# Attention and routed experts on one core: row operations from GpSimd to VectorE, and a slots' table read in two parts

## The chip, the core and the metric

The kernel runs on one core of a Trainium2 chip, as one program. The metric is the device time of one execution in microseconds (us); the time of a kernel is the median of its runs.

## What is computed

The reference first computes a linear attention without softmax, on 8 batches and 8 heads with 576 tokens of width 64, normalises each output row by its root mean square and scales it by `g_norm`. The 4608 rows of 512 numbers then go through a layer of 8 experts: each token goes to the expert with its largest logit, an expert takes at most `capacity` (1152) tokens in order, and each kept token's result is weighted by its gate.

```python
kv = np.einsum('bhsd,bhse->bhde', k, v)
out = np.einsum('bhsd,bhde->bhse', q, kv)
rms = np.sqrt(np.mean(out * out, axis=-1, keepdims=True) + 1e-06)
x = (out / rms * g_norm)                      # as rows of 512
...
expert_idx = np.argmax(x @ w_gate, axis=1)    # tokens of an expert in order, up to capacity
h = np.maximum(np.einsum('ecd,edf->ecf', disp, w1), 0.0)      # 512 -> 1024
y = np.einsum('ecf,efd->ecd', h, w2)                          # 1024 -> 512
out[i] = gate_w[i] * y[expert_idx[i], pos[i]]
```

## The kernel before, in words

The program has two plans, emitted one after the other. A planner (`Plan`, L97) takes operations with a planned duration, a list of engines that may do them, dependencies, a key and rings of buffers (`Ring`, L82, with `Hold`s). It simulates the engines and places, at each step, the operation with the lowest key among those that can start first; `late` moves an operation's earliest start back. The order that it finds is the order of each engine's instructions. The engines then run in that order, each waiting only for its real dependencies, so an instruction that waits holds up all that is behind it on its engine. GpSimd's and SP's DMA issues are part of their orders.

**First plan: attention and routing.** For each of the 8 batches TensorE makes k-v products and the outputs, ScalarE and VectorE copy them out of PSUM, and `route` (L866) finds each token's expert and its position there. With a product (`enter`, L1007) it writes the token's number into a table in PSUM, `tab`: column = expert and block of 128 positions (48 columns, once for the high and once for the low bits), partition = position within the block. `x_dram` gets the unnormalised rows with the row's factor and gate. After the third batch one expert is picked (`pick`, L1058) and its weights are loaded and split. After the fifth batch `early_slots` (L1146) reads the table (`read_table`, L1094) for that expert's first 384 slots, and `early_products` (L1241) computes their first expert layer. `finish` (L1274) reads the table again after the last batch, cuts the indices of the first expert's other slots (`slots`, L634: a register load, then a copy of the expert's six columns of `gidx_tab`, the rows to gather, and of `sidx_tab`, the rows to write) and ranks the experts by their number of tokens (`rank_experts`, L1071), so that each of the following experts gets a fixed budget of slots (704, 672, 640, 624, 592, 576, 560, 512).

`read_table` has eight operations of VectorE over 128x48: two put high and low bits together, one (L1098) sets slots beyond the capacity to 0, and `slot_rows` (L312) makes from token + 1 the row to gather (0 where the slot is empty) and the row to write (beyond the last row where it is empty).

**Second plan: the experts.** `rows_beside` (L1577) prepares the rows of expert r + 1 while expert r is computed: an indirect DMA issued by GpSimd gathers 128 rows (`xg`, L438, four buffers), `norm` (L442) multiplies them by their factors into `xm`, ScalarE rounds `xm` to f16 (`pair_high`, L469), `pair_low` (L474) makes the f16 rest, and a transposing DMA on SP's queue (L481) writes both into `xs`. For the second expert `norm` may be on VectorE or GpSimd; for the third expert on it is on GpSimd, as `pair_low` is for all. `weights` (L1526) loads an expert's two weight matrices in four parts each (SP's queue, L326) and splits them into f16 high and low parts: VectorE takes the largest magnitude of each of 8 pieces (L342, `am`), `most` reduces them and multiplies by `gcol` for the first matrix (L352), TensorE turns the column (`across`, L355, tile `pt_max`), VectorE reduces it (L359), TensorE spreads the number to all partitions (`back`, L362), VectorE makes the power of two (`scale`, L364 to L371), then ScalarE writes the high parts (L376) and VectorE the low parts (L382, `w1l` and `w2l`). `products` (L1612) computes an expert: eight groups of products into `hp` (L530, two buffers in PSUM), ScalarE's `hh` (L535), VectorE's `hl` (L538), then the second layer by blocks of 128 rows (L576, narrow ones L585 to L596), ScalarE's scaling into `ysb` (L601, three buffers) and GpSimd's indirect DMA to the output (L606). `hl` and other operations of the expert at hand have the key of one expert before, and `pt_max` has the lowest key of all (FIRST).

During the last expert VectorE runs the steps of `plan_rest` (L1331, 68 places for them), which prepare a part that is only run when an expert has more tokens than its budget.

## Time and profile before

| | us |
|---|---|
| median of 3 runs | 569.93 (567.73 to 570.16) |
| the profiled execution | 566.6 |
| its span, first to last instruction | 564.8 |
| TensorE busy | 520.2 (92%) |
| VectorE busy | 382.5 (68%) |
| ScalarE busy | 252.7 (45%) |
| GpSimd busy | 207.1 (37%) |
| mean granted TensorE clock | 0.981 of full |

The profile's lines name the engines PE (TensorE's products; PEld its weight loads), DVE (VectorE), ACT (ScalarE), POOL (GpSimd) and SP (SyncE; SPq its DMA queue). L576 is line 576 of the kernel before. `out<-in` are tile names, followed by shapes; `x8` counts instructions that were merged into one line. A bracket at the end of a line tells how long the engine had been idle before it and what ended the wait. Durations of neighbouring instructions overlap slightly, so the busy time of a merged line is less than their number times the duration of one.

### The profile page before, as it was taken

The numbers are of one execution on the slowest core, as the hardware profiler recorded it, in microseconds if no ns is written. First come the engines' busy times: TensorE is split into PE (matmuls) and PEld (weight loads), VectorE is DVE, ScalarE is ACT, GpSimd is POOL, SyncE is SP. The second block draws the span as 40 slices with busy tenths as digits, with TensorE's granted clock in tenths as the row PEclk, the third lists the DMA queues.
The fourth block names the chain that finished last, engine by engine and source line by source line (L and its number), as shares of the span: only waits on it lengthen the run. The fifth ranks groups of instructions, "written<-read, shape, count | busy, mean of one in ns | idle before, by whom it ended". The sixth has DMA issues, their size and how long they took to land.

```text
span 564.8 us, 12345 instructions
## 1 busy us (share of the span) xinstructions
PE 520.2 (92%) x4727; PEld 343.2 (61%) x4727; DVE 382.5 (68%) x978; ACT 252.7 (45%) x508; POOL 207.1 (37%) x233
## 2 busy tenths in 40 slices
PE   4989897978979997998999999999999999999995
PEld 4878786855536564544664575487467648745442
DVE  4468899899949979999997286367729606721200
ACT  1748684876313661644633526252544525202210
POOL 3011013552255684755225640644373171012011
PEclk9979996999999998999999999999999999999999
DMA  8999999592277687795938562664666151001001
GB/s 278 376 354 301 384 390 373 176 317 96 96 232 254 144 302 166 201 306 132 277 109 236 112 224 66 169 171 161 167 140 214 39 114 39 1 38 40 0 30 40
DMA packets 78020, 102.60 MB, mean 182 GB/s; under 512 B 43222, under 2 KB 51414, under 8 KB 76932
## 3 DMA queue, kind: packets, MB, share of 16 engines
q1 hardware_dynamic: 69600, 70.43, 42.5%
q0 software_dynamic: 7776, 31.30, 15.6%
q8 instruction: 39, 0.64, 0.5%
q14 instruction: 25, 0.20, 0.1%
q10 hardware_dynamic: 580, 0.02, 0.1%
HBM read 73.13 MB, written 20.61 MB: 166 GB/s over the span
## 4 chain that ended last, share of the span: by engine, by line
PE 26%; issue 16%; DMA 5%; DVE 3%; POOL 1%; ACT 1%; POOLq 0%; DVEq 0%; ACTq 0%
PE yp L576 12%; PE hp L530 12%; DMA out_dram<-ysb,si 5%; DVE w2l L382 1%; PE yp L585 1%; POOL xg L438 1%; DVE hl L538 1%; ACT w1h L376 0%; ACT w2h L376 0%; POOL xm L446 0%; POOLq L1652 0%; POOL pair L476 0%; POOL out_dram L606 0%; PE pt_max L355 0%; PE pt_max L362 0%
## 5 line engine op out<-in xcount | busy, mean ns | idle before, releaser
L530 PE MATMUL hp<-xs,w1h 128*128 128x320 f16 (+6 forms) x896 | 134.4, 301 | 5.1 <-DVE hl L538 4.5
L530 PEld LDWEIGHTS <-w1h 128*128 128x128 f16 x960 | 93.4, 98 | 47.1 <-issue 8.8
L576 PEld LDWEIGHTS <-hh 128*128 128x128 f16 x560 | 54.4, 98 | 65.5 <-issue 2.9
L606 POOL DMA_INDIRECT out_dram<-ysb,si x41 | 42.8, 1043 | 137.3 <-ACT ysb L601 99.6
L535 ACT ACTIVATE hh<-hp 128x320 f16<-128x320 f32 (+7 forms) x64 | 40.8, 638 | 114.5 <-PE hp L530 111.9
L342 DVE TENSOR_REDUCE am<-raw 128x1 f32<-128x512 f32 x120 | 75.6, 673 | 4.1 <-DMA raw<-in_moe_w_dram 3.8
L530 PE MATMUL hp<-xs,w1l 128*128 128x320 f16 (+6 forms) x448 | 72.0, 301 | 0.0
L538 DVE SCALAR_TENSOR_TENSOR hl<-hp,hh 128x320 f16<-128x320 f32 (+7 forms) x64 | 47.2, 737 | 32.9 <-ACT hh L535 32.8
L476 POOL TENSOR_TENSOR pair<-xm,pair 128x512 f16<-128x512 f32 (+5 forms) x35 | 44.7, 1278 | 66.5 <-ACT pair L472 61.8
L576 PE MATMUL yp<-w2h,hh 128*128 128x512 f16 x272 | 64.4, 379 | 0.8 <-ACT ysb L601 0.8
L576 PE MATMUL yp<-w2l,hh 128*128 128x512 f16 x272 | 64.6, 379 | 0.0
L576 PE MATMUL yp<-w2h,hl 128*128 128x512 f16 x272 | 64.3, 379 | 0.0
L601 ACT ACTIVATE ysb<-yp,ysc 128x512 f32<-128x512 f32 (+5 forms) x40 | 27.3, 684 | 82.4 <-PE yp L576 73.1
L382 DVE SCALAR_TENSOR_TENSOR w2l<-raw,sw,w2h 128x512 f16<-128x512 f32 x64 | 53.8, 885 | 10.7 <-ACT w2h L376 9.9
L530 PEld LDWEIGHTS <-w1l 128*128 128x128 f16 x480 | 46.9, 98 | 19.5
L438 POOL DMA_INDIRECT xg<-x_dram,gi x41 | 42.3, 1031 | 40.1 <-DVE gi L640 27.0
L382 DVE SCALAR_TENSOR_TENSOR w1l<-raw,sg,w1h 128x512 f16<-128x512 f32 x64 | 47.5, 797 | 0.9 <-ACT w1h L376 0.8
L576 PEld LDWEIGHTS <-hl 128*128 128x128 f16 x280 | 27.0, 98 | 31.9
L823 PE MATMUL op<-kv_bd,qt 128*128 128x144 f32 x256 | 42.6, 310 | 3.7 <-ACT qt L676 1.3
L376 ACT ACTIVATE w2h<-raw,sw 128x512 f16<-128x512 f32 x62 | 39.8, 711 | 5.2 <-DVE p2t L307 2.1
L376 ACT ACTIVATE w1h<-raw,sg 128x512 f16<-128x512 f32 x60 | 38.3, 711 | 7.2 <-DVE sg L371 7.1
L823 PEld LDWEIGHTS op<-kv_bd,qt 128*128 128x128 f32 x256 | 36.7, 206 | 6.0 <-ACT qt L676 2.2
(246 smaller groups left out, 688.7 us busy)
## 6 DMA issues: line engine op xcount, KB each, us to landing
raw<-in_moe_w_dram SPq DMA_DIRECT2D x64, 512.0 KB
k_sb<-in_k_dram SPq DMA_DIRECT2D x16, 576.0 KB
v_sb<-in_v_dram SPq DMA_DIRECT2D x16, 576.0 KB
x_dram<-o_sb POOLq DMA_DIRECT2D x8, 1152.0 KB
q_sb<-in_q_dram SPq DMA_DIRECT2D x16, 512.0 KB
x_dram<-o_sb POOLq DMA_DIRECT2D x8, 144.0 KB
q_sb<-in_q_dram SPq DMA_DIRECT2D x32, 32.0 KB
xg<-x_dram,gi POOLq DMA_INDIRECT x41
```

Of the source, the lines that this page charges most:

```text
L342: nc.vector.tensor_reduce(out=am()[:, p:p + 1], in_=raw[:, sl(p)], axis=AX.X, op=ALU.max, apply_absolute_value=True)
L376: nc.scalar.activation(wh[:, sl(p)], raw[:, sl(p)], AF.Copy, scale=z["s"])
L382: nc.vector.scalar_tensor_tensor(out=wl[:, sl(p)], in0=raw[:, sl(p)], scalar=z["s"], in1=wh[:, sl(p)], op0=ALU.mult, op1=ALU.subtract)
L438: nc.gpsimd.indirect_dma_start(out=self.xg[i][0:n], out_offset=None, in_=x_dram[0:self.rows, :], in_offset=bass.IndirectOffsetOnAxis(ap=se ...
L476: nc.gpsimd.tensor_tensor(out=pair[0:n, 1], in0=self.xm[i][0:n], in1=pair[0:n, 0], op=ALU.subtract)
L530: nc.tensor.matmul(self.view(hp)[:, u], lhsT=w[:, c, j * P:(j + 1) * P], rhs=x[:, c, u * hw:(u + 1) * hw], start=(t == 0 and c == 0), stop ...
L535: nc.scalar.activation(self.out(self.hh, j), self.view(hp), AF.Relu)
L538: nc.vector.scalar_tensor_tensor(out=self.out(self.hl, j), in0=self.view(hp), scalar=0.0, in1=self.out(self.hh, j), op0=ALU.max, op1=ALU.s ...
L576: nc.tensor.matmul(yp[0:n, 0:DM], lhsT=h[:, j, o:o + n], rhs=w[:, j, :], start=(m == 0), stop=(m == len(self.terms) - 1))
L601: nc.scalar.activation(self.ysb[0:n], yp[0:n, 0:DM], AF.Copy, scale=self.ysc[0:n, i:i + 1])
L606: nc.gpsimd.indirect_dma_start(out=out[:, :], out_offset=bass.IndirectOffsetOnAxis(ap=self.sidx[0:n, col:col + 1], axis=0), in_=ysb[0:n], ...
L823: nc.tensor.matmul(y, lhsT=qt.t[:, i * P:(i + 1) * P], rhs=kv2[:, half * HH + i], start=True, stop=True)
```

## The change

From the third expert on `norm` and `pair_low` are given to VectorE, with planned times of 0.64 us, and the planner may place such a `norm` no earlier than 3.0 us (LANDED) after the gather is expected. The `pt_max` products get `late` of 5.0 and 3.0 us in place of 2.0 and 1.0. The two scalings by `gcol` take it as a per-partition scalar in place of a second tensor.

`read_table` now stops after three operations, at the rows to gather; slots beyond the capacity are no longer set to 0 there, and `targets` adds a number beyond the last row for them (`past`, made once at the start) when it makes the rows to write, in three operations later. `slots` takes the tables one at a time and can reuse a register; `finish` reuses the one loaded in `early_slots`. `rank_experts` loses one operation and hands three others (`last_e`, `cmp`, `bud_e`) to the first steps of `plan_rest`, which has 71 places.

```diff
+LANDED = 3.0
...
-    slot_pos = cst.tile([P, W], F32, name="slot_pos")
-    nc.gpsimd.iota(slot_pos, [[0, E], [P, NHI]], base=0, channel_multiplier=1, allow_small_or_imprecise_dtypes=True)
+    past = cst.tile([P, W], F32, name="past")
+    nc.gpsimd.iota(past, [[0, E], [P, NHI]], base=0, channel_multiplier=1, allow_small_or_imprecise_dtypes=True)
...
             if i == 0:
-                nc.vector.tensor_tensor(out=a1, in0=a1, in1=gcol, op=ALU.mult)
+                nc.vector.tensor_scalar(out=a1, in0=a1, scalar1=gcol, scalar2=None, op0=ALU.mult)
...
-                nc.vector.tensor_tensor(out=sg, in0=z["s"], in1=gcol, op=ALU.mult)
+                nc.vector.tensor_scalar(out=sg, in0=z["s"], scalar1=gcol, scalar2=None, op0=ALU.mult)
...
-        def pair_low(self, i):
+        def pair_low(self, i, eng=nc.gpsimd):
             n, pair = self.part(i)[1], self.pair[i]
-            nc.gpsimd.tensor_tensor(out=pair[0:n, 1], in0=self.xm[i][0:n], in1=pair[0:n, 0], op=ALU.subtract)
-            nc.gpsimd.engine_nop()
+            eng.tensor_tensor(out=pair[0:n, 1], in0=self.xm[i][0:n], in1=pair[0:n, 0], op=ALU.subtract)
+            if eng is nc.gpsimd:
+                nc.gpsimd.engine_nop()
...
     def columns(e):
...
+        nc.vector.tensor_scalar(out=past, in0=past, scalar1=cap, scalar2=BIG, op0=ALU.is_ge, op1=ALU.mult)
...
-        nc.vector.tensor_scalar(out=perm, in0=perm, scalar1=float(NHI), scalar2=None, op0=ALU.mult)
-        nc.vector.tensor_copy(perm_i[:, 1], perm)
-        nc.vector.tensor_copy(last_e, eq[:, E - 1])
-        nc.vector.tensor_tensor(out=cmp, in0=eq, in1=outer(rbud), op=ALU.mult)
-        nc.vector.tensor_reduce(out=bud_e, in_=cmp.rearrange("p r e -> p e r"), axis=AX.X, op=ALU.add)
+        nc.vector.tensor_scalar(out=perm_i[:, 1], in0=perm, scalar1=float(NHI), scalar2=None, op0=ALU.mult)
+        early["by_rank"] = eq, cmp, outer(rbud)
 
     def read_table():
-        t = sm.tile([P, W], F32, name="tab_sb", bufs=1)
-        nc.vector.tensor_copy(t, tab[:, W:2 * W])
+        early["tab"] = t = sm.tile([P, W], F32, name="tab_sb", bufs=1)
+        nc.vector.tensor_scalar(out=t, in0=tab[:, W:2 * W], scalar1=-1.0, scalar2=None, op0=ALU.add)
         nc.vector.scalar_tensor_tensor(out=t, in0=tab[:, 0:W], scalar=64.0, in1=t, op0=ALU.mult, op1=ALU.add)
-        nc.vector.scalar_tensor_tensor(out=t, in0=slot_pos, scalar=cap, in1=t, op0=ALU.is_lt, op1=ALU.mult)
-        slot_rows(t, gidx_tab, sidx_tab, W)
+        nc.vector.tensor_scalar(out=gidx_tab, in0=t, scalar1=0.0, scalar2=None, op0=ALU.max)
+
+    def targets():
+        t = early["tab"]
+        tw = sm.tile([P, W], F32, name="tw", bufs=1)
+        nc.vector.tensor_scalar(out=tw, in0=t, scalar1=0.0, scalar2=BIG, op0=ALU.is_lt, op1=ALU.mult)
+        nc.vector.tensor_tensor(out=tw, in0=tw, in1=past, op=ALU.add)
+        nc.vector.tensor_tensor(out=sidx_tab, in0=tw, in1=t, op=ALU.add)
...
     def early_slots():
-        o = op(("V", 1.9), lambda e: read_table(), enters[-1:], key)
-        readers.setdefault("tab", []).append(o)
+        t = op(("V", 0.75), lambda e: read_table(), enters[-1:], key)
+        readers.setdefault("tab", []).append(t)
         def cut(e):
-            early["gi"], early["si"] = slots(ep, first_i[0:1, 1:2])
-        o = op(("V", 0.6), cut, [o] + early["picked"], key)
+            early["first"] = {"c": nc.vector.value_load(first_i[0:1, 1:2], min_val=0, max_val=(E - 1) * NHI)}
+            early["gi"], = slots(ep, early["first"], ("gi",))
+        def cut2(e):
+            targets()
+            early["si"], = slots(ep, early["first"], ("si",))
+        o = op(("V", 0.7), cut, [t] + early["picked"], key)
+        early["slots2"] = [op(("V", 0.6), cut2, [t, o], key)]
...
     def finish():
-        o = op(("V", 1.9), lambda e: read_table(), enters[-1:] + early["slots"], key)
+        o = op(("V", 0.75), lambda e: read_table(), enters[-1:] + early["slots"] + early["slots2"], key)
         def cut(e):
-            early["gi0"], early["si0"] = slots(ep, first_i[0:1, 1:2], EARLY)
-        early["cut"] = o2 = op(("V", 0.8), cut, [o], key)
+            early["gi0"], = slots(ep, early["first"], ("gi",), EARLY)
+        def cut2(e):
+            targets()
+            early["si0"], = slots(ep, early["first"], ("si",), EARLY)
+        early["cut"] = o = op(("V", 0.2), cut, [o], key)
+        o2 = op(("V", 0.6), cut2, [o], key + 0.2)
         o = count(cnt_all, key)
-        early["rank"] = op(("V", 3.4), lambda e: rank_experts(cnt_all), [o, o2], key + 0.1)
+        early["rank"] = op(("V", 2.5), lambda e: rank_experts(cnt_all), [o], key + 0.1)
+        early["cut2"] = o2
...
-            o = op(("T", 0.12), across, [o], FIRST, (x,), late=2.0)
+            o = op(("T", 0.12), across, [o], FIRST, (x,), late=5.0)
...
-            o = op(("T", 0.06), lambda e, f=f, x=x: f["back"](x.t[:, 0:1]), [o], FIRST, (), (x,), late=1.0)
+            o = op(("T", 0.06), lambda e, f=f, x=x: f["back"](x.t[:, 0:1]), [o], FIRST, (), (x,), late=3.0)
...
-            a = op([("V", 0.61), ("P", NORM)] if r == 1 else ("P", NORM),
-                   lambda e, i=i: st["x"].norm(i, nc.vector if e == "V" else nc.gpsimd), [o], key - 5 if r == 1 else key + 1,
-                   (xm,), (xg,))
+            a = op([("V", 0.61), ("P", NORM)] if r == 1 else ("V", 0.64),
+                   lambda e, i=i: st["x"].norm(i, by_letter[e]), [o], key - 5 if r == 1 else key + 1,
+                   (xm,), (xg,), late=0.0 if r == 1 else LANDED)
...
-            a = op(("P", PAIR), lambda e, i=i: st["x"].pair_low(i), [a], key + 1, (), (xm, pair, hold))
+            a = op(("P", PAIR) if r == 1 else ("V", 0.64), lambda e, i=i: st["x"].pair_low(i, by_letter[e]), [a], key + 1, (),
+                   (xm, pair, hold))
```

(In the last lines r = 1 is the second expert.)

## Rows read from the trace of the kernel before

**Rows 1.** Busy by stage: stretch, PE, PEld, DVE, ACT, POOL, clock, DMA, GB/s.

```profile
100.00:154.00 54.00, 46.39 (x461) 33.03 (x459) 52.23 (x157) 36.36 (x96) 21.53 (x20) 1.00 0.50 170
...
200.00:270.00 70.00, 63.15 (x448) 37.05 (x449) 65.28 (x115) 35.08 (x58) 42.94 (x46) 0.98 0.77 226
...
371.00:421.00 50.00, 49.98 (x402) 32.65 (x400) 31.71 (x67) 21.16 (x35) 22.69 (x26) 1.00 0.61 160
```

**Rows 2.** Waits of TensorE in the whole span: total, times, longest.

```profile
PE hp L530 <- DVE hl L538: 4.5, 3, 3.7
```

**Rows 3.** TensorE's timeline, 205 to 290 us: start, us, instruction.

```profile
217.85 3.73 PE L530 MATMUL hp<-xs,w1h 128*128 128x336 f16 x16 [3.70 <-DVE hl L538]
...
221.37 1.73 PE L530 MATMUL hp<-xs,w1l 128*128 128x336 f16 x8
...
222.94 2.44 PE L530 MATMUL hp<-xs,w1h 128*128 128x336 f16 x16
...
225.22 1.30 PE L530 MATMUL hp<-xs,w1l 128*128 128x336 f16 x8
...
255.19 0.27 PE L355 MATMUL pt_max<-ident,a 128*1 128x128 f32 x1 [0.47 <-DVE a L352]
...
258.35 0.16 PE L362 MATMUL pt_max<-bm,ones_bf 1*128 1x1 bf16 x1 [1.16 <-DVE bm L359]
...
265.64 0.16 PE L362 MATMUL pt_max<-bm,ones_bf 1*128 1x1 bf16 x1 [1.07 <-DVE bm L359]
```

**Rows 4.** VectorE's timeline in the same stretch.

```profile
209.82 6.62 DVE L382 SCALAR_TENSOR_TENSOR w2l<-raw,sw,w2h 128x512 f16<-128x512 f32 x2
...
216.96 0.84 DVE L538 SCALAR_TENSOR_TENSOR hl<-hp,hh 128x672 f16<-128x672 f32 x1
...
252.26 2.88 DVE L352 TENSOR_TENSOR a<-a,gcol 128x1 f32<-128x1 f32 x1
...
260.53 2.66 DVE L371 TENSOR_TENSOR sg<-sw,gcol 128x1 f32<-128x1 f32 x1
```

**Rows 5.** GpSimd's timeline in the same stretch.

```profile
209.69 1.07 POOL L446 TENSOR_TENSOR xm<-xg 128x512 f32<-128x512 f32 x1
...
213.13 2.09 POOL L446 TENSOR_TENSOR xm<-xg 128x512 f32<-128x512 f32 x2
...
253.02 2.09 POOL L446 TENSOR_TENSOR xm<-xg 128x512 f32<-128x512 f32 x2
```

**Rows 6.** VectorE's groups by line and shape, 320 to 350 us.

```profile
L382 DVE SCALAR_TENSOR_TENSOR w2l<-raw,sw,w2h 128x512 f16<-128x512 f32 x8 | 5.6, 750 | 9.9 <-ACT w2h L376 9.9
...
L371 DVE TENSOR_TENSOR sg<-sw,gcol 128x1 f32<-128x1 f32 x1 | 0.2, 159 | 0.0
```

**Rows 7.** The same view, 199 to 270 us, VectorE and GpSimd.

```profile
L382 DVE SCALAR_TENSOR_TENSOR w2l<-raw,sw,w2h 128x512 f16<-128x512 f32 x16 | 17.4, 1142 | 0.8 <-issue 0.8
...
L476 POOL TENSOR_TENSOR pair<-xm,pair 128x512 f16<-128x512 f32 x9 | 10.4, 1159 | 9.5 <-ACT pair L472 9.4
...
L446 POOL TENSOR_TENSOR xm<-xg 128x512 f32<-128x512 f32 x9 | 9.5, 1061 | 0.3 <-issue 0.2
```

**Rows 8.** Timelines around the first expert's rows, and ScalarE's first `w1h`.

```profile
154.38 0.21 DVE L1096 COPY tab_sb<-tab 128x48 f32<-128x48 f32 x1 [0.90 <-PE tab L1009]
...
156.72 0.17 DVE L640 COPY gi<-gidx_tab 128x6 int32 x1 [0.58 <-issue]
...
167.94 0.68 DVE L446 TENSOR_TENSOR xm<-xg 64x512 f32<-64x512 f32 x1 [2.21 <-DMA xg<-x_dram,gi]
...
157.76 1.03 POOL L438 DMA_INDIRECT xg<-x_dram,gi  x1 [0.47 <-issue]
...
159.85 4.91 SPq L326 DMA_DIRECT2D raw<-in_moe_w_dram  x6
...
169.37 0.43 PE L458 MATMUL xp<-ident,xm 64*128 64x64 f32 x4 [2.74 <-DVE gt L453]
...
184.64 0.72 ACT L376 ACTIVATE w1h<-raw,sg 128x512 f16<-128x512 f32 x1 [1.02 <-DVE sg L371]
```

More of the change, by code (lines that the diff above doesn't have):

```diff
@@ L1334, in plan_rest @@
         cnt = cnt_all
+        eq, cmp, by_rank = early["by_rank"]
+        nc.vector.tensor_copy(last_e, eq[:, E - 1])
+        yield
+        nc.vector.tensor_tensor(out=cmp, in0=eq, in1=by_rank, op=ALU.mult)
+        yield
+        nc.vector.tensor_reduce(out=bud_e, in_=cmp.rearrange("p r e -> p e r"), axis=AX.X, op=ALU.add)
+        yield
         kept = mw.tile([P, E], F32, name="kept")
@@ L1581, in cut @@
         def cut(e):
-            st["gi"], st["si"] = slots(mo, perm_i[0:1, 1, r:r + 1])
-        cut_ = op(("V", 0.4), cut, [early["rank"]], key, (sl,))
+            st["gi"], st["si"] = slots(mo, perm_i[0:1, 1, r:r + 1], ("gi", "si"))
+        cut_ = op(("V", 0.4), cut, [early["rank"], early["cut2"]], key, (sl,))
         n = len(spans(0, BUDGET[r]))
```

28 lines of the change are left out of this document (14 added, 14 removed).

## The prediction

> **What bounds the kernel now.** I read the table by stage first [rows 1]. In the stretch from 371 to 421 us TensorE is busy 49.98 us of 50, and so it goes from the fourth expert (near 320 us) to the tail: there nothing that another engine does shows in the time, and the change can win only before that. Between 200 and 270 us, where the second expert's products run, TensorE loses 6.85 us of 70 and VectorE is busy 65.28; between 100 and 154 us VectorE is busy 52.23 of 54. Then the waits of TensorE: the longest in the experts' part is for `hl` on VectorE [rows 2]. Third, TensorE's timeline [rows 3]: one hole of 3.70 us before 217.85, three short ones (0.47, 1.16 and 1.07 us) before `pt_max`. Fourth, what VectorE did in them [rows 4]: at 209.82 two `w2l` operations take 6.62 us and the next `hl` starts only at 216.96; at 252.26 an operation on one column takes 2.88 us and at 260.53 another 2.66. In those moments GpSimd runs its row operations back to back [rows 5] (two lows of 1.17 and 1.15 us lie between the first two), and they belong to the third and fourth experts. Undisturbed, later in the same trace, eight `w2l` take 5.6 us (0.70 each) and the one-column operation 0.159 us [rows 6]. So VectorE stands still while GpSimd computes: this, and not VectorE's work as such, makes `hl` late.
>
> The hole carries a price of its own. After it the granted clock fell: the table's clock column is below 1 for this stretch [rows 1], and the first group of 16 and of 8 products takes 3.73 and 1.73 us where the next takes 2.44 and 1.30 [rows 3]. That is 1.29 + 0.43 = 1.7 us more, the level of 1.2 GHz for some microseconds.
>
> **The change part by part.** The sum is made against the profiled execution, 566.6 us with a span of 564.8; the runs shown have a median of 569.93, 3.3 us above, so the difference is carried over to the median.
>
> *Row operations to VectorE.* Between 199 and 270 us GpSimd does nine full norms, nine full lows and one short one of each [rows 7]: 20 operations, all of the third and fourth experts. On VectorE the norm costs 0.68 us [rows 8]; the low (f32 and f16 in, f16 out) has no row there, its nearest is `w2l` at 0.70 with the same types [rows 6], and the end below is the norm's 0.68. So 20 times 0.68 is 13.6 us of new work. What goes: the 16 `w2l` took 17.4 us [rows 7] where 16 times 0.70 is 11.2, so 6.2; and 2.72 + 2.50 from the two one-column operations, in all 11.4 us. Net VectorE gains 2.2 us of work in a stretch where 4.7 us were idle. None of the moved operations is urgent: the third expert's rows are needed when its products begin, right after the `pt_max` of 265.64 [rows 3], the fourth's a whole expert later, while `hl` has its place by the planner's lowest key. So the hole and its clock go: −3.70 − 1.72 = −5.4 us. Ends: −5.4 and 0. For the added work I take +0.7, a third of the 2.2, ends 0 and +2.2. Later experts get 10 operations each, 6.8 us on top of VectorE's 31.71 of 50 [rows 1]: TensorE's products hide them, cost nothing. If that cover were gone, each would be 0.68 us on TensorE's path.
>
> What queues behind what: a norm on VectorE waits for its gather, and `hl` may stand behind it; LANDED puts 3.0 us between, where the planner had only its 1.1. In the one place where VectorE already does norms it waited 2.21 us for a gather [rows 8]. On GpSimd the fifth fetch now waits for VectorE's norm of the first tile (the buffer is the same), and the output writes stand behind it; three output buffers cover that. On SP the transposes, and the weight loads behind them, wait for VectorE's low instead of GpSimd's.
>
> *The `pt_max` products and the two scalings.* The planner now puts them 3 and 2 us later in TensorE's order, and the scalings by `gcol` become operations with one tensor input. The three short holes are 2.70 us [rows 3], and their causes, the 2.88 and 2.66 us, go with GpSimd's work: −2.7, ends −2.7 and 0. The price is that a weight's scale is known up to 5 us later. From the third expert on that is hidden: the scaling at 260.53 belongs to the fourth expert, used only after the third's products. For the second expert it is not: its first `w1h` starts at 184.64 [rows 8], its products near 200 us, and eight highs and eight lows lie between. They can still fit, since VectorE takes the next load's maxima first, so +0.5, ends 0 and +5.0.
>
> *The slots' table.* From the first table operation at 154.38 to `gi` at 156.72 there are 2.34 us, 0.58 of them the register load [rows 8]: eight operations in 1.76 us, 0.22 each. Three operations and no register load give 0.66, so `gi` comes 1.7 us earlier. But the first gather is at 157.76 because an output write stands before it on GpSimd, which was emitted with the first plan and waits for ScalarE; earlier indices alone don't move it. The ranks come earlier too, by 1.6 us or so, and with them the six weight loads at 159.85 on SP, which run beside the gathers; the last gather's norm started at 167.94 and TensorE waited 2.74 us until 169.37 [rows 8]. Earlier loads can delay these gathers, earlier maxima help the second expert. I take 0, ends −1.7 and +1.7. The first reading of the table, near 100 us, loses two of eight operations: −0.4 where VectorE is nearly full [rows 1], ends −1.0 and +1.0, since the planner reorders this part. The targets, the budgets (three operations moved into the last experts' 71 steps) and one operation more at the start lie where VectorE has idle time: 0.
>
> Sum: −5.4 + 0.7 − 2.7 + 0.5 + 0 − 0.4 = −7.3 us. On the profiled execution 559.3; on the median **562.6 us**.
>
> **A rule against the row.** The row shows two `w2l` held for 6.62 us [rows 4] while five GpSimd operations of about 1.1 us passed [rows 5]. The Trainium skill (SBUF — State Buffer, Who interferes with whom) says that a VectorE instruction with two SBUF inputs contends with a GpSimd instruction that reads SBUF, and that the loser blocks until the other's instruction is finished. By it the two operations would lose at most one GpSimd operation each, some 2.3 us (an estimate with this trace's durations) and not 6.62 − 1.40 = 5.2; the trace agrees on who blocks whom, and differs on how long. With 2.3 in place of the 5.4 the page's sum would be −4.2; I keep to the row.
>
> **The rivals.** *Given back* (0.18). The two engines only swap the load. From 205 to 217 us VectorE would do four norms and two lows itself, six times 0.68 = 4.1 us in place of the 5.2 lost, so `hl` is 1.1 us earlier and no more; the hole stays at 2.6 us and the clock falls all the same. Sum −1.1 − 2.7 + 0.5 − 0.4 = −3.7, so 566.2. Against it: the moved operations stand behind `hl` in the planner's order of keys, so they need not fall before it. The Trainium skill (Perfetto Trace Analysis, Optimizing Scalar/DVE Operations) says that moving work between VectorE and GpSimd might not help since they share a read port; the rows of this trace speak for a gain, because what is lost there is standstill and not bandwidth.
>
> *The second expert's weights late* (0.10). If the later scale reaches TensorE, the second expert's products start 5.0 us later and the clock falls as at 217.85 (1.7): −7.3 − 0.5 + 6.7 = −1.1, so 568.8. For it: only some 15 us lie between the first `w1h` [rows 8] and its use; against it: VectorE's work there is only put in another order.
>
> *VectorE becomes the bound* (0.07), the case on the other side. If the long operations are not GpSimd's doing, 13.6 us come on top of 65.28 in a stretch of 70: 8.9 us that do not fit, and nothing is won at 217.85 or at `pt_max`: 569.9 + 8.9 − 0.4 = 578.4. It decides at 200 to 270 us, from the point where VectorE's work passes what is left beside `hl`; short `w2l` in every stretch without GpSimd speak against it.
>
> That GpSimd keeps the rows after all is excluded: from the third expert on the list of engines has one entry.
>
> **How the numbers follow.** The forecast has 0.65. A measurement of this kernel can tell about 0.5%, 2.85 us, from no change: 567.1 and 572.8. All best ends give −5.4 − 2.7 − 1.7 − 1.0 = −10.8, 559.1, and the runs differ by 1.2 to 2.2 us from their median: low 557.5. The high end, 569.0, takes in the first two rivals and leaves out the third and part of the second. Faster 0.62 from the forecast, 0.11 from the first rival, 0.02 from the second: 0.75. Same 0.16, slower 0.09 (0.07 from the last rival, the rest from reordering).
>
> **What would show it.** Right: no hole near 214 us, `w2l` at 0.70 us in all stretches, clock 1.00 from 200 on, no `pt_max` wait above 0.5 us, TensorE's losses between 200 and 270 under 2 us. Wrong: a wait of `hp` for `hl` with a norm waiting for its gather before it, a hole at the second expert's first products, or a longer wait at the first expert's rows near 165 us.

## The result, and the profile after

The changed kernel takes 565.22 us (median of 20 executions) against 569.71 us before (20), a ratio of 0.9915 with a 95% interval of 0.9894 to 0.9936: 4.5 us faster, where 7.3 were forecast. The profiled execution has a span of 562.1 us against 564.8. A second series of the same kernel, told below, gave another number, and that is part of the answer. Where a trace comes from an execution away from its kernel's median, only the stretch around the edit is read.

The table by stage, as in [rows 1], with the fourth expert's stretch added (stretch, PE, PEld, DVE, ACT, POOL, clock, DMA, GB/s):

```profile
100.00:154.00 54.00, 46.43 (x462) 35.10 (x461) 51.44 (x160) 38.57 (x102) 23.01 (x22) 0.97 0.51 183
200.00:270.00 70.00, 70.00 (x581) 43.78 (x578) 65.16 (x132) 34.90 (x57) 22.93 (x28) 1.00 0.80 224
320.00:371.00 51.00, 47.61 (x359) 30.05 (x358) 40.64 (x86) 22.56 (x37) 12.00 (x12) 1.00 0.59 158
```

Between 200 and 270 us TensorE loses nothing at all, and the clock is 1.00; GpSimd's 42.94 us have become 22.93. VectorE's busy time is what it was, 65.16 against 65.28, though it does twenty row operations more (the two windows don't hold quite the same work, since the changed kernel is ahead at 270 us). But in the stretch from 320 to 371 us, where the kernel before lost nothing, 3.39 us are gone.

VectorE's groups between 199 and 270 us, which answer to [rows 7]: the 16 `w2l` take 745 ns each instead of 1142, and the rows' two operations 0.68 each.

```profile
L380 DVE SCALAR_TENSOR_TENSOR w2l<-raw,sw,w2h 128x512 f16<-128x512 f32 x16 | 10.9, 745 | 0.2 <-ACT w2h L374 0.2
...
L474 DVE TENSOR_TENSOR pair<-xm,pair 128x512 f16<-128x512 f32 x9 | 6.0, 681 | 0.0
L444 DVE TENSOR_TENSOR xm<-xg 128x512 f32<-128x512 f32 x9 | 5.9, 683 | 0.0
```

Where did the gain go? The first product of each expert, read from TensorE's timeline (us), shows it:

| | first | second | third | fourth | fifth | span |
|---|---|---|---|---|---|---|
| before | 171.47 | 199.60 | 265.74 | 319.65 | 371.17 | 564.8 |
| after | 175.09 | 202.45 | 259.20 | 313.36 | 368.80 | 562.1 |
| after minus before | +3.62 | +2.85 | −6.54 | −6.29 | −2.37 | −2.7 |

The second expert's stretch, from its first product to the third expert's, falls from 66.14 to 56.75 us: 9.39 won. Besides the four holes of [rows 3] the kernel before had one more there, before its second product, for the expert's rows; it is gone too:

```profile
200.45 2.30 PE L530 MATMUL hp<-xs,w1h 128*128 128x336 f16 x15 [0.53 <-DMA xs<-pair]
```

The first expert begins 3.62 late, and the fourth's stretch grows from 51.52 to 55.44: 3.92 given back. The rest, −0.8 between the first and second and some tenths later, is small: 3.62 − 0.77 − 9.39 + 0.25 + 3.92 − 0.33 = −2.7.

The hole in the fourth expert, on TensorE's, VectorE's and GpSimd's timelines:

```profile
323.43 2.28 PE L529 MATMUL hp<-xs,w1h 128*128 128x312 f16 x16 [3.34 <-DVE hl L537]
...
316.42 0.15 DVE L641 COPY gi<-gidx_tab 128x6 int32 x1
321.91 0.17 DVE L641 COPY si<-sidx_tab 128x6 int32 x1 [5.34 <-DMA out_dram<-ysb,si]
...
322.59 0.79 DVE L537 SCALAR_TENSOR_TENSOR hl<-hp,hh 128x624 f16<-128x624 f32 x1
...
314.41 2.93 POOL L605 DMA_INDIRECT out_dram<-ysb,si  x1 [4.40 <-ACT ysb L600]
```

`hl` is late as in [rows 2], but VectorE isn't busy: it waits 5.34 us with a copy of six columns. The copy fills one of three `si` tiles, and the oldest is still read by an output write issued at 314.41 and not yet landed; `hl` stands behind the copy.

The first expert's rows, which answer to [rows 8] (VectorE, GpSimd, SP, TensorE):

```profile
158.11 0.21 DVE L1095 TENSOR_SCALAR tab_sb<-tab 128x48 f32<-128x48 f32 x1 [1.93 <-PE tab L1011]
...
166.90 0.69 DVE L444 TENSOR_TENSOR xm<-xg 128x512 f32<-128x512 f32 x1 [4.84 <-DMA xg<-x_dram,gi]
...
158.88 1.06 POOL L605 DMA_INDIRECT out_dram<-ysb,si  x1 [8.99 <-DVE gidx_tab L1097]
160.25 1.03 POOL L436 DMA_INDIRECT xg<-x_dram,gi  x1 [0.30 <-issue]
...
154.57 4.51 SPq L324 DMA_DIRECT2D raw<-in_moe_w_dram  x6
...
167.69 0.85 PE L456 MATMUL xp<-ident,xm 128*128 128x128 f32 x4 [2.85 <-issue]
```

The table is read at 158.11 instead of 154.38, though its reading is short now; the six loads of weights are issued from 154.57, ahead of the gathers and no longer behind them; the first norm waits 4.84 us for its gather.

### The profile page after: what moved, and what is told of

It reads as the page before. It is cut to its first block, busy times and chain, and to the rows that moved or that the text cites. A ratio compares the mean times of both kernels' runs of the same rounds, so it can differ in the third digit from the quotient of the medians.

```text
span 562.1 us, 12278 instructions
## 1 busy us (share of the span) xinstructions
PE 521.2 (93%) x4727; PEld 344.3 (61%) x4727; DVE 396.8 (71%) x1030; ACT 254.0 (45%) x509; POOL 146.1 (26%) x176
## 4 chain that ended last, share of the span: by engine, by line
PE 43%; issue 19%; DMA 18%; DVE 15%; ACT 2%; POOL 1%; SPq 0%; POOLq 0%; DVEq 0%; ACTq 0%
PE hp L529 17%; PE yp L575 14%; DMA out_dram<-ysb,si 12%; PE op L825 3%; DMA q_sb<-in_q_dram 3%; DMA raw<-in_moe_w_dram 2%; DVE ss L858 2%; PE qp L807 2%; DVE am L340 1%; DMA v_sb<-in_v_dram 1%; PE a L736 1%; PE yp L584 1%; DVE w1l L380 1%; DVE hl L537 1%; PE op L575 1%
## 5 line engine op out<-in xcount | busy, mean ns | idle before, releaser
L605 POOL DMA_INDIRECT out_dram<-ysb,si x41 | 45.6, 1111 | 253.2 <-ACT ysb L600 208.5
L575 PE MATMUL yp<-w2h,hh 128*128 128x512 f16 x272 | 65.7, 383 | 0.6 <-ACT ysb L600 0.6
L436 POOL DMA_INDIRECT xg<-x_dram,gi x41 | 43.0, 1050 | 38.6 <-DVE am L340 13.5
L825 PE MATMUL op<-kv_bd,qt 128*128 128x144 f32 x256 | 44.2, 320 | 4.5 <-DVE hi_i L986 3.0
L380 DVE SCALAR_TENSOR_TENSOR w1l<-raw,sg,w1h 128x512 f16<-128x512 f32 x64 | 45.4, 751 | 1.8 <-ACT w1h L374 1.6
L380 DVE SCALAR_TENSOR_TENSOR w2l<-raw,sw,w2h 128x512 f16<-128x512 f32 x64 | 44.9, 747 | 0.2 <-ACT w2h L374 0.2
L825 PEld LDWEIGHTS op<-kv_bd,qt 128*128 128x128 f32 x256 | 38.7, 215 | 6.5 <-issue 3.9
L470 ACT CAST pair<-xm 128x512 f16<-128x512 f32 (+5 forms) x35 | 21.2, 614 | 26.7 <-DMA xs<-pair 18.2
```

The lines of the kernel that those rows point to most:

```text
L380: nc.vector.scalar_tensor_tensor(out=wl[:, sl(p)], in0=raw[:, sl(p)], scalar=z["s"], in1=wh[:, sl(p)], op0=ALU.mult, op1=ALU.subtract)
L436: nc.gpsimd.indirect_dma_start(out=self.xg[i][0:n], out_offset=None, in_=x_dram[0:self.rows, :], in_offset=bass.IndirectOffsetOnAxis(ap=se ...
L470: nc.scalar.copy(self.pair[i][0:n, 0], self.xm[i][0:n])
L575: nc.tensor.matmul(yp[0:n, 0:DM], lhsT=h[:, j, o:o + n], rhs=w[:, j, :], start=(m == 0), stop=(m == len(self.terms) - 1))
L605: nc.gpsimd.indirect_dma_start(out=out[:, :], out_offset=bass.IndirectOffsetOnAxis(ap=self.sidx[0:n, col:col + 1], axis=0), in_=ysb[0:n], ...
L825: nc.tensor.matmul(y, lhsT=qt.t[:, i * P:(i + 1) * P], rhs=kv2[:, half * HH + i], start=True, stop=True)
```

## The experiments

The experiments were measured in three series, on three chips: `rows_only`, `no_rows`, `si4` and `rank_after`; then `changed_again`, `fetch_later`, `loads_after` and `rows_fetch_later`; then `gather_only`, `early_norms` and the two with wasted work on GpSimd. Each ratio is to the kernel before in the same series (567.96, 566.65 and 568.92 us), and kernels of two series are compared by their ratios.

### Which part won the second expert's 9.4 us

`rows_only`: the kernel before, and of the change only the row operations (with their planned landing time).

```diff
-            a = op([("V", 0.61), ("P", NORM)] if r == 1 else ("P", NORM),
+            a = op([("V", 0.61), ("P", NORM)] if r == 1 else ("V", 0.64),
...
-            a = op(("P", PAIR), lambda e, i=i: st["x"].pair_low(i), [a], key + 1, (), (xm, pair, hold))
+            a = op(("P", PAIR) if r == 1 else ("V", 0.64), lambda e, i=i: st["x"].pair_low(i, by_letter[e]), [a], key + 1, (),
```

> Only the row operations of the third expert and later move to VectorE; the table, the ranks and the pt_max products stay as before. Theory (VectorE stood still while GpSimd computed; the table's part of the change cost time at the first expert): TensorE loses under 2 us between 200 and 270 us, w2l is 0.75 us or less there, the granted clock is 1.00; the first expert's first product stays near 171.5 us as before, the third expert's starts 7 to 9 us earlier than before (257 to 259 us), and the whole is 5 to 8 us faster than before, about 1 to 1.4%. Rival (the gain comes from the later pt_max products and the scaling with one tensor input): the hole near 214 us and the long one-column operations stay, and the time is within 2 us of before.

Measured: 564.43 us, ratio 0.9954 [0.9924, 0.9983]. The second expert's stretch is 57.99 us (before 66.14), `w2l` 745 ns, the third expert's first product at 261.74. The rival falls: the row operations alone win the stretch. The whole won 3.5 us, less than the 5 expected, and the third expert begins later than expected, because of a hole before the second expert. TensorE waits there for VectorE's copy `yt`, and VectorE had been idle for 2.68 us before that copy, with all that the profile shows of its inputs done:

```profile
203.12 0.60 PE L598 MATMUL yp<-ident,yt 128*64 128x128 f32 x4 [3.47 <-DVE yt L593]
```

`no_rows`: the changed kernel, row operations back on GpSimd (the same two lines reversed, and no planned landing time).

> The changed kernel with norms and lows from the third expert on back on GpSimd. Theory (standstill): w2l operations of over 2 us between 200 and 225 us come back, with a hole of 2 to 5 us before hp and a clock below 1.00; the second expert's stretch gives back 6 to 9 us of its gain, the table's part still costs the first expert 3.5 us, so the time is 4 to 9 us above the changed kernel and at or above before. Rival (the pt_max part made the gain): within 2 us of the changed kernel.

Measured: 572.75 us, ratio 1.0085 [1.0051, 1.0118]. The total is about as the theory had it, but the reason isn't: the second expert's stretch takes only 57.42 us, with no hole in it. VectorE and GpSimd still hold each other up, only elsewhere. VectorE's timeline, then GpSimd's:

```profile
243.44 4.04 DVE L380 SCALAR_TENSOR_TENSOR w1l<-raw,sg,w1h 128x512 f16<-128x512 f32 x6
...
250.76 10.09 DVE L380 SCALAR_TENSOR_TENSOR w2l<-raw,sw,w2h 128x512 f16<-128x512 f32 x8
...
266.29 0.21 DVE L350 TENSOR_SCALAR a<-a,gcol 128x1 f32<-128x1 f32 x1
```

```profile
243.34 6.11 POOL L444 TENSOR_TENSOR xm<-xg 128x512 f32<-128x512 f32 x2
...
258.18 2.12 POOL L444 TENSOR_TENSOR xm<-xg 128x512 f32<-128x512 f32 x2
...
265.75 1.06 POOL L444 TENSOR_TENSOR xm<-xg 112x512 f32<-112x512 f32 x1
```

Two norms of GpSimd take 6.11 us where two take 2.12 a little later: this time GpSimd stands, while VectorE does `w1l` after `w1l`. At 250.76 it is VectorE's turn: eight `w2l` in 10.09 us where [rows 6] has eight in 5.6. Neither shows in the time, because no `hl` was due behind them. So the rows' move is enough for this stretch (`rows_only`), and in this trace the stretch is as short without it, since the collision falls where nothing waits. What moved it there isn't shown: the other part of the change (later `pt_max`, scaling with one tensor input, another order) may have, but so may the 6 us for which TensorE stood just before this stretch (told below), in which GpSimd had already issued its first four gathers, while in the kernel before they were issued after the expert's first product. No run has the other part alone without such a standstill.

Before the fourth expert of this kernel the collision does cost time. Eight `w1l` take 1.21 us each in the mean (the longest 3.05), VectorE is late for the fourth expert's products, and the clock falls as at 217.85 in the kernel before:

```profile
332.25 3.47 PE L529 MATMUL hp<-xs,w1h 128*128 128x312 f16 x16 [2.22 <-DVE p2t L308]
```

The fourth's stretch takes 55.88 us, against 51.83 in `rows_only`. VectorE also waited 0.92 us there for a load, so not all of it is the collision. The larger part of the 10.8 us between this trace (572.9 us) and the changed kernel's (562.1) lies before the second expert's first product (212.51 against 202.45): the first expert begins 3.70 us later, and its stretch takes 33.72 us instead of 27.36.

### Is it GpSimd's reading that stops VectorE?

Both kernels are `fetch_later` (below), the fastest that was found, with wasted work on GpSimd after each tile of rows of the third and fourth experts: 20 products of old SBUF tiles, or 20 fills.

```diff
+            for _ in range(2 if r in (2, 3) else 0):
+                nc.gpsimd.tensor_tensor(out=old[0][:, DM:2 * DM], in0=old[0][:, 0:DM], in1=old[1][:, 0:DM], op=ALU.mult)
...
+                nc.gpsimd.memset(old[0], 0.0)
```

> The kernel with both mends, and on GpSimd, after each tile of rows of the third and fourth experts, two wasted products of two old SBUF tiles (128x576 f32), 20 in all beside the second expert's products. Theory (VectorE's operations with two SBUF inputs stand still while GpSimd reads SBUF): the w2l operations between 200 and 270 us rise from 0.745 us to 1.0 or more in the mean, hl (one input in PSUM), the maxima and the scaling with one tensor input keep their 0.85, 0.61 and 0.21 us. Whether TensorE sees it depends on what stands behind: 0 to 6 us more. Rival (VectorE was slow for its own reasons): w2l stays at 0.75.

> The same with two fills of an old SBUF tile (128x1152 f32) in place of the wasted products: GpSimd is as busy but reads nothing. By the Trainium skill's page SBUF (GpSimd contends when it reads SBUF), and the theory that goes with it, w2l stays at 0.75 us and the time is that of the kernel without them. Rival (any work of GpSimd holds VectorE): w2l as long as with the wasted products.

VectorE's and GpSimd's groups, 199 to 271 us, with the reading products:

```profile
L380 DVE SCALAR_TENSOR_TENSOR w2l<-raw,sw,w2h 128x512 f16<-128x512 f32 x16 | 11.6, 784 | 0.0
L380 DVE SCALAR_TENSOR_TENSOR w1l<-raw,sg,w1h 128x512 f16<-128x512 f32 x11 | 9.9, 939 | 0.8 <-ACT w1h L374 0.8
L474 DVE TENSOR_TENSOR pair<-xm,pair 128x512 f16<-128x512 f32 x9 | 9.4, 1061 | 0.0
L537 DVE SCALAR_TENSOR_TENSOR hl<-hp,hh 128x672 f16<-128x672 f32 x8 | 6.8, 845 | 1.4 <-ACT hh L534 1.4
...
L1611 POOL TENSOR_TENSOR kv_bd<-kv_bd,kv_bd 128x512 f32<-128x512 f32 x20 | 28.5, 1424 | 0.8
```

and with the fills:

```profile
L380 DVE SCALAR_TENSOR_TENSOR w2l<-raw,sw,w2h 128x512 f16<-128x512 f32 x16 | 10.9, 744 | 0.2 <-ACT w2h L374 0.2
L380 DVE SCALAR_TENSOR_TENSOR w1l<-raw,sg,w1h 128x512 f16<-128x512 f32 x10 | 7.0, 741 | 0.8 <-ACT w1h L374 0.8
...
L474 DVE TENSOR_TENSOR pair<-xm,pair 128x512 f16<-128x512 f32 x9 | 5.9, 678 | 0.0
...
L1611 POOL MEMSET kv_bd<- 128x1152 f32 x20 | 21.2, 1060 | 0.6
```

With the fills the weights' and the rows' operations on VectorE are as short as without them, though GpSimd is busy 21 us. With the products `w1l` goes from 741 to 939 ns and the rows' low from 678 to 1061; `w2l` rises only to 784, not the 1.0 expected, as 13 of the 16 fall where no product runs; `hl`, whose one input lies in PSUM, keeps its 0.85. From the second expert's first product to the end it takes 364.5 us (563.8 − 199.34) with the products, 357.1 (554.2 − 197.06) with the fills and 357.2 (563.3 − 206.11) in `fetch_later`, whose trace is late only before that product: the products cost 7.4 us, the fills nothing. In medians it is 562.99 (six executions) against 557.36 us (two). For these operations the rival (any work of GpSimd) falls.

One operation doesn't fit the theory, the small scaling `ysc`, which has one tensor input and a scalar per partition. With the products, then with the fills:

```profile
L566 DVE TENSOR_SCALAR ysc<-gt,ys 128x5 f32<-128x5 f32 x2 | 2.3, 1166 | 0.1
...
L566 DVE TENSOR_SCALAR ysc<-gt,ys 128x5 f32<-128x5 f32 x2 | 1.1, 558 | 0.1
```

In the changed kernel its mean is 0.27 us. The long one of each trace (1.93 us at 268.72, 0.89 us at 262.15) has the wasted work beside it, the first also a copy and a DMA issue of GpSimd. What holds it wasn't tested.

### The hole in the fourth expert

`si4`: the changed kernel with a fourth `si` buffer. The order of the instructions is the same.

```diff
-            t = pool.tile([P, NHI + 1], I32, name=f"{nm}{s0}", bufs=3)
+            t = pool.tile([P, NHI + 1], I32, name=f"{nm}{s0}", bufs=4 if nm == "si" else 3)
```

> The changed kernel with four buffers instead of three for the targets' indices (si), nothing else; the order of instructions is the same. Theory (the copy into si waits for the output write of the expert three before, and hl stands behind it): the waits of 2.83 us at 272.7 and 5.34 us at 321.9 on VectorE are gone, the holes of 0.52 and 3.34 us before hp with them, so the fourth expert's last products end 3.5 to 4 us earlier and the whole is about 3.9 us faster than the changed kernel (0.7%). Rival (VectorE's seven or so added operations per expert make hl late, the wait is only idle time): holes of the same size stay near 273 and 323 and the time is within 1 us of the changed kernel.

The copy no longer waits, and the stretch from 320 us on is full (VectorE's timeline, then the table by stage):

```profile
323.08 0.15 DVE L641 COPY si<-sidx_tab 128x6 int32 x1
```

```profile
320.00:371.00 51.00, 51.00 (x377) 32.37 (x376) 42.23 (x89) 22.76 (x36) 16.54 (x14) 1.00 0.64 180
```

The fourth expert's stretch is 51.74 us (before 51.52, after 55.44): the theory holds there, 3.7 us. Yet the whole was no faster than the changed kernel: 566.37 us, 0.9965 [0.9937, 0.9992]. Its second expert began at 207.46 us and not at 202.45.

### The standstill near 200 us

In `si4` TensorE stood for 6 us in the 64-column products of the first expert's last tile. `changed_again` is the changed kernel once more.

> The changed kernel as it is, a second time, on the chip and beside the runs of the next three. In the four-buffer kernel TensorE stood in its 64-column products (yp<-hh,w2h of the first expert's last tile) for 6 us, issuing two to five of them every 0.75 us; in the changed kernel's first trace the same order of instructions ran through in 2.9 us. If the standstill is chance from run to run, this trace may show it, and the changed kernel's spans should spread over some 6 us; if it belongs to the four-buffer kernel, the trace shows it at most briefly and the third expert's first product is near 259 us again.

Measured: 572.30 us in six executions (570.96 to 577.27), ratio 1.0121 [1.0073, 1.0169] to before on the same chip: the kernel that won 4.5 us in one series loses 5.7 in another (566.65 before, there). All six are above all twenty of the first series (561.41 to 567.92), so it isn't chance from one execution to the next; what differs between the series wasn't tested. TensorE's timeline and GpSimd's:

```profile
199.39 0.40 PE L584 MATMUL yp<-hl,w2h 128*128 128x64 f16 x8
199.62 0.37 PE L584 MATMUL yp<-hh,w2l 128*128 128x64 f16 x7
200.21 0.19 PE L584 MATMUL yp<-hh,w2l 128*128 128x64 f16 x1 [0.22 <-issue]
...
200.93 0.22 PE L584 MATMUL yp<-hh,w2h 128*128 128x64 f16 x2 [0.45 <-issue]
201.66 0.23 PE L584 MATMUL yp<-hh,w2h 128*128 128x64 f16 x2 [0.51 <-issue]
...
206.03 0.23 PE L584 MATMUL yp<-hh,w2l 128*128 128x64 f16 x1 [0.49 <-issue]
...
207.58 4.24 PE L529 MATMUL hp<-xs,w1h 128*128 128x336 f16 x16
```

```profile
198.81 1.25 POOL L436 DMA_INDIRECT xg<-x_dram,gi  x1 [0.18 <-issue]
...
204.26 0.96 POOL L436 DMA_INDIRECT xg<-x_dram,gi  x1 [0.30 <-issue]
```

Eight products pass in 0.23 us, then one to five every 0.73 us, for 6 us, and they wait for nothing that the profile shows. It starts as GpSimd's first gather for the third expert ends (198.81 + 1.25) and stops 0.8 us after its last (204.26 + 0.96). The granted clock falls to 0.50, the level of 1.2 GHz, from 204.4 to 211.2 us: the next 16 products take 4.24 us, not 2.45. TensorE wasn't waiting for its instructions to be loaded, as far as the DMA view shows: from 198 to 204 us it lists no packet of an instruction queue. The changed kernel's first trace has the same order and no standstill. Of the 7.8 us between the two traces (569.9 and 562.1) the first expert's stretch is 6.1 (33.48 against 27.36) and the second's 1.8 (58.54 against 56.75). `fetch_later` moves one instruction of `si4`, the first of these gathers, behind the output write:

```diff
+                early[r, "narrow"] = o
...
-            o = op(("P", 1.05), fetch, [cut_, first] + early.get(("lows", r - 1), [])[-1:], key, (hold, xg), (sl,))
+            o = op(("P", 1.05), fetch, [cut_, first] + early.get(("lows", r - 1), [])[-1:] + ([early[0, "narrow"]] if r == 2 else []), key, (hold, xg), (sl,))
```

> The four-buffer kernel in which one instruction moves: the third expert's first gather stands behind the next output write on GpSimd, some 1.3 us later; all other orders are the same. Theory (TensorE's standstill at the 64-column products comes from GpSimd's gathers that run beside them; it began when the first gather ended and ended 1.0 us after the last): the 64-column products now end before the first gather does, no product is held, the second expert's first product is at 201 to 203 us instead of 207.5, the granted clock stays 1.00 from there on, and the whole is 4 to 7 us faster than the four-buffer kernel. Rival (the standstill is set by the loads of weights or by something else): it is there in the same size and the time is within 1.5 us of the four-buffer kernel.

Measured: 558.26 us, ratio 0.9868 [0.9822, 0.9914], the best without wasted work (the traced execution took 565.14; its last table product is at 161.6, 3.9 us later than in the changed kernel's). TensorE's and GpSimd's timelines: the products end before the first gather starts, none is held, and 16 take 2.45 us. The three other kernels with the later gather and this order (`gather_only` and the two with wasted work) show no standstill there either.

```profile
205.68 0.40 PE L584 MATMUL yp<-hh,w2l 128*128 128x64 f16 x8
...
206.11 2.45 PE L529 MATMUL hp<-xs,w1h 128*128 128x336 f16 x16
...
204.52 1.53 POOL L605 DMA_INDIRECT out_dram<-ysb,si  x1 [1.24 <-ACT ysb L600]
206.35 1.00 POOL L436 DMA_INDIRECT xg<-x_dram,gi  x1 [0.30 <-issue]
```

`gather_only` has the later gather and again three `si` buffers.

> The changed kernel with three buffers for si as it is, and the third expert's first gather behind the next output write (the kernel with the later gather, without the fourth buffer). Theory (two separate losses: gathers beside the 64-column products, and the si copy that waits for an old output write): no standstill near 200 us, clock 1.00 there, but the waits of the si copy and the hole of 3 us or so before hp in the fourth expert are back; the time is 3 to 4.5 us above the 558.3 us of the kernel with both, and 8 us or more below the changed kernel's 572.3 of the last call. Rival (the fourth buffer alone, or where the program lies, made that kernel fast): a standstill near 200 us and 565 us or more.

Measured: 566.03 us, 0.9984 [0.9944, 1.0023]. No standstill (the second expert begins at 201.41 with 2.45 us for 16 products), and the fourth's hole is back, with a price on the clock: 3.68 us, and 3.95 us for 16 products where after had 2.28.

```profile
323.76 3.95 PE L529 MATMUL hp<-xs,w1h 128*128 128x312 f16 x16 [3.68 <-DVE hl L537]
```

So there are two losses, each mended by its own edit: the changed kernel's second series has both, `si4` only the standstill, `gather_only` only the hole, `fetch_later` neither. The hole cost 1.2% by the ratios of the two series, 6.6 us, and 5.5 by the traces (57.24 against 51.73 us for the fourth's stretch), more than the 3 to 4.5 expected, since the clock falls too; and the time is 6.3 us below 572.3, not 8.

`rows_fetch_later` does the same to `rows_only`; in its order it is the third gather that moves.

> The kernel before with only the row operations moved to VectorE, and the third expert's third gather behind the output write. Theory (gathers hold TensorE or its signals near 200 us): the 3.5 us in which nothing ended between 199.6 and 203.1 us are gone or under 1 us, and the time is 3 to 5 us below the kernel with only the row operations moved, near 560 us. Rival (not the gathers): the same hole and the same time within 1.5 us.

Measured: 563.03 us, ratio 0.9954 [0.9922, 0.9985], the same as without the move. The hole of 3.5 us is gone from the trace (from the first expert's first product to the third's 86.2 us instead of 89.4), but the time doesn't show it. This one stays undecided.

### The first expert's start

`rank_after`: in the changed kernel the ranks wait for the first cut again, as before.

```diff
-        early["rank"] = op(("V", 2.5), lambda e: rank_experts(cnt_all), [o], key + 0.1)
+        early["rank"] = op(("V", 2.5), lambda e: rank_experts(cnt_all), [o, early["cut"]], key + 0.1)
```

> The changed kernel with the rank of the experts kept behind the first cut of the indices, as it was before the change. Theory (the ranks, now free of the table, are placed ahead of it on VectorE, and with them the loads of weights ahead of the gathers on the DMA queues): the last table product is 2 to 4 us earlier than the changed kernel's 157.7, the first expert's gathers are issued ahead of the weights' loads, the first norm waits under 2.5 us instead of 4.84, and the first expert's first product is near 171.5 us instead of 175.1; the whole is 2 to 4 us faster than the changed kernel unless the second expert's weights, now later, take it back. Rival (the late start comes from the attention part alone): the first expert's first product stays within 1 us of 175.1 and the time is that of the changed kernel.

Measured: 576.08 us, 1.0159 [1.0109, 1.0210]: the time went the other way, by the standstill (second expert at 211.32) and the `si` wait, and the first expert begins at 174.94, not 171.5. On the way the first half of the theory holds: from the last attention product to the last table product it takes 25.1 us, as before (25.0), where the changed kernel takes 26.1 and 28.9 in its two traces. The second half holds only for the first gather, which is issued ahead of the loads and whose norm doesn't wait; then an output write came between the gathers, the loads ahead of the second, and its norm waited longer than ever:

```profile
155.66 0.21 DVE L1095 TENSOR_SCALAR tab_sb<-tab 128x48 f32<-128x48 f32 x1 [1.16 <-PE tab L1011]
...
169.91 0.69 DVE L444 TENSOR_TENSOR xm<-xg 128x512 f32<-128x512 f32 x1 [6.38 <-DMA xg<-x_dram,gi]
```

`loads_after`: `si4`, with the ranks written to the loads' table only after the first gather has landed.

```diff
-        nc.vector.tensor_copy(perm_i[:, 0], perm)
-        nc.vector.tensor_scalar(out=perm_i[:, 1], in0=perm, scalar1=float(NHI), scalar2=None, op0=ALU.mult)
+        early["perm"] = perm
...
+    early["rank"] = op(("V", 0.3), perm_out, [early["rank"], gates[0]], -KEY)
```

> The four-buffer kernel in which the ranks reach the table of the loads only after the first expert's first gather has landed, so that no load of the second expert's weights stands ahead of the first expert's gathers. Theory (the gathers took 6 to 7 us because the loads went ahead of them): the three gathers land within 4.5 us of their issue, the first norm waits under 3 us, the first expert's first product comes 3 us or more after the last table product than now (15 to 16 us instead of 17.2 to 18.5 in the kernels with early loads); the price is that the second expert's weights come 5 us later or more, and TensorE may wait for them near 200 us. Rival (the gathers are slow by themselves behind the output write): the same 17 to 18.5 us from the last table product to the first expert's first product.

VectorE's timeline and SP's:

```profile
161.76 0.69 DVE L444 TENSOR_TENSOR xm<-xg 128x512 f32<-128x512 f32 x1 [4.14 <-DMA xg<-x_dram,gi]
...
163.24 0.69 DVE L444 TENSOR_TENSOR xm<-xg 128x512 f32<-128x512 f32 x1 [0.56 <-DMA xg<-x_dram,gi]
...
163.47 5.00 SPq L324 DMA_DIRECT2D raw<-in_moe_w_dram  x6
```

The first norm still waits 4.14 us, not under 3, but it starts 3.8 us after its gather was issued (157.93), where the changed kernel needs 6.7 (160.25 to 166.90). The second gather's norm waits 0.56 us, and the first expert's first product is at 168.86, 13.5 us after the last table product (155.38) where `si4` needs 18.7 and the kernel before 17.5: in these traces gathers without loads ahead of them or beside them are worth 4 to 5 us. But the second expert starts at 204.88. The weights that come later aren't the reason, as far as the trace shows: of the 3.3 us that TensorE loses between 172 and 200 us, half are waits for VectorE near 175 us and the rest is a standstill in the last 64-column products, and then comes a hole like that of `rows_only`, with VectorE idle for 4.39 us before the copy:

```profile
204.05 1.03 PE L595 MATMUL yp<-ident,yt 128*64 128x128 f32 x4 [4.01 <-DVE yt L590]
```

In all 566.21 us, 0.9987 [0.9955, 1.0018]: won first, lost after.

### The same collision in the attention part

`early_norms`: `fetch_later`, with the norms of the early rows on VectorE too.

```diff
-            a = op([("V", 0.61), ("P", 1.05)], lambda e, i=i: st["rows"].norm(i, nc.vector if e == "V" else nc.gpsimd), [o],
+            a = op(("V", 0.61), lambda e, i=i: st["rows"].norm(i, nc.vector if e == "V" else nc.gpsimd), [o],
```

> The kernel with both mends (four buffers, later gather), and the norms of the first expert's early rows, near 120 us, also on VectorE. Theory (there too VectorE stood still beside GpSimd's norms: an operation of 0.16 us took 2.21): the hole of 3.0 us before op at 123 us is gone, and the time is 1 to 3 us below 558.3. Rival (VectorE is nearly full in that part, 50 us of 54, so 2 us more work there come out as time): 0 to 3 us above 558.3.

Measured: 563.36 us, 0.9918 [0.9886, 0.9950], by the ratios 0.5% slower than `fetch_later`, where the theory had it faster. The 2.21 us operation is back to 0.16 and the hole before `op` falls from 3.0 to 1.0 us; the first expert begins at 169.80. But the planner's new order put the gathers beside the 64-column products again, and a standstill of 3 us is back, with a slow clock behind it. Inconclusive as to its worth.

## Why the prediction was right, and where it was wrong

**The direction and the place** were right: 565.22 lies in the range, the gain is in the second expert's stretch, and it shows as foretold (no hole near 214 us, clock 1.00, no `pt_max` wait, TensorE's losses under 2 us; 16 `w2l` busy for 10.9 us, 0.68 each, by the count that gave 0.70). **The size there** was low: the terms −5.4, +0.7, −2.7 and +0.5 make −6.9, measured −9.4. The +0.7 for VectorE's added work isn't there: the twenty operations cost 13.3 us, as counted, shorter `w2l` and one-column operations give back 12.2, and TensorE sees nothing of the rest. Nor is the +0.5 for late weights, and the hole of 0.53 us at 200.45 wasn't listed. **That the total lies in the range** is in part luck: this stretch won 2.5 us more than its terms, two other places lost 7.5, and in its second series the same kernel is slower than before.

**"So the hole and its clock go"** was argued from the rows' move alone, and `rows_only` bears it out. What I had not seen is that the hole can also go with the rows still on GpSimd (`no_rows`): VectorE's standstill costs only where `hl` stands behind it.

**"TensorE's products hide them, cost nothing"** holds for the operations: `rows_only` has them, and its fourth stretch is 51.83 us. What failed is that nothing else was charged to the later experts: the order that the planner found for the whole change cost 3.9 us there. It put the next expert's cut at 316.42, ahead of an `hl`, and the cut waits for the landing of a write, which the plan counts as done when it is issued. I had asked what queues behind a norm and looked at the output's three buffers, not at `si`'s three. So the sign of being wrong that I named, `hp` waiting for `hl`, is there, but with a copy and not a norm before it.

**"I take 0, ends −1.7 and +1.7"** for the table failed, +3.6 and outside both ends; the longer wait at the first expert's rows, named as a sign, is the 4.84 us at 166.90. One reading was wrong: the output write ahead of the first gather waited for VectorE's table and not for ScalarE, as its line before shows,

```profile
156.22 1.07 POOL L606 DMA_INDIRECT out_dram<-ysb,si  x1 [6.40 <-DVE sidx_tab L320]
```

so the short reading did move the gather, from 3.38 to 2.14 us after the table's first operation. I let the ranks come earlier by the table's saving; freed from the table they were placed ahead of it, and the last table product came at 157.70 instead of 153.97, all of the 3.6. The loads on SP ran ahead of the gathers with them (the plan has them behind, but nothing at run time holds SP there; before, the late ranks did); that took back what the short reading won, since from the last table product to the first expert's first product it is 17.4 us, and was 17.5. How much of the 3.7 is the attention part's own is open: its last product is at 129.1 us before and at 131.8 and 127.9 in the changed kernel's two traces, which leaves 1.1 or 3.9 for the ranks.

**The rule against the row.** The Trainium skill (SBUF — State Buffer, Who interferes with whom) was right on who contends, for the weights' and the rows' operations: one with two SBUF inputs, and only against a GpSimd instruction that reads (products against fills). By one GpSimd instruction lost per operation the stretch would have won 3.8 us of the −4.2, far from 9.4; the row's longer standstill was the better guide. That the whole, −4.5, lies near −4.2 is chance, since the losses elsewhere are in it.

**The rivals.** Part of the gain was given back, but at other places than that rival had it. VectorE did not become the bound. `changed_again` looks like the second expert's weights coming late (start 5 us late, clock down), but TensorE stood in products that use the first expert's weights: that rival's mechanism was not seen in the changed kernel. And "a measurement can tell 0.5%" was too bold: two series of this kernel differ by 7 us. The standstill explains the difference of the two traces; that its presence is what separates all executions of the two series was not shown.

## What to carry to other kernels

When two engines hold each other up, ask which instruction stands behind the one that is held: busy time doesn't tell whether the collision costs anything, the instruction behind it does. When an edit lets a planner move steps earlier, list what each now waits for that was long done before: a ring of buffers released by a transfer's landing, a queue whose place was kept only by a late input. And trace a kernel twice before believing a difference of one per cent.

## What the runs showed of the hardware that was not expected

- GpSimd can be the one that stands: two norms in 6.11 us, against 2.12, beside VectorE's `w1l` one after the other. One side's operations follow each other while the other waits for several of them.
- The length of the held operation doesn't matter: one of a single column took 2.88 us [rows 4]; with one tensor input in place of two it took 0.21 with GpSimd's norm beside it (266.29 in `no_rows`). That isn't so for each operation with one tensor input: `ysc` once took 1.93 us.
- TensorE's standstill at 64-column products: in `changed_again`, `si4`, `no_rows`, `rank_after`, `loads_after` and `early_norms` it came where GpSimd's indirect transfers ran beside them, and moving one gather took it away (four traces); in the changed kernel's first trace they ran beside each other without it. In `rows_only` and `loads_after` VectorE's copy behind these products started only after VectorE had been idle for 2.68 and 4.39 us. What holds them stays open.
